# Turning B and C of eight pairs with crossbar DMAs on the sync queue instead of TensorE transposes

## The chip, the cores and the metric

The kernel runs on one core of one Trainium2 chip. The metric is the device time of one execution, in microseconds (us), as the median of several executions. With one core there is no second die to compare with, so an execution counts as "slow" when it is over 1.5% above the fastest of the same kernel. Comparisons use the others, the "fast" ones. Every ratio below is the mean time of one kernel's fast runs over the mean time of the other's fast runs of the same rounds, so it is not quite the ratio of the medians that stand beside it.

A profiled execution has a span a little shorter than the device time (125.4 us against 127.1). All times read from profiles count from the start of that span.

## The reference

A state-space layer (Mamba-2 style, in chunks) is followed by a gated feed-forward layer. Cut to what matters here:

```python
x: (4, 8, 768, 32)   a: (4, 8, 768)   B, C: (4, 8, 768, 16)    # batch, heads, tokens, ...
for each chunk of tokens:
    CB      = C @ B^T                      # per head, tokens x tokens
    y_intra = (CB * L) @ x                 # L: causal decays
    y_inter = (C @ state) * decay
    state   = decay_full * state + B^T @ (x * decay)
y -> 3072 tokens x 256
out = (relu(y @ w_gate) * (y @ w_val)) @ w_out     # 256 -> 1536 -> 256
```

`CB` sums over the 16 state columns, and a matmul sums over partitions. So B and C, loaded with tokens on the partitions, have to be turned until head and state lie on the partitions.

## The kernel before

The 3072 tokens are cut into 12 pairs of 128-token chunks and into 6 blocks of 512 tokens. Attention of pair P = 2b+2 and Q = 2b+3 is woven into the feed-forward matmuls of block b. Each engine works through its instructions in program order, and so does the sync queue (SP), which issues nearly all DMAs. The parts that matter:

```python
def load(p):                         # six DMAs on the sync queue for pair p >= 3
    q = nc.sync
    ...
    for i in range(2):               # two chunks
        for src, j in ((B, 0), (C, 1)):
            q.dma_start(out=bcr[:, i, j], in_=src[b, :, sl, :].rearrange("h s n -> s h n"))
        q.dma_start(out=xr[:, i], in_=x[b, :, sl, :].rearrange("h s d -> s h d"))

def scale_bc(p, eng):                # GpSimd: decay factors into B and C, cast to bf16
    bs = att.tile([128, 4, 128], BF16, tag="bs", name="bs")
    for t in range(2):
        eng.tensor_tensor(out=bs...[:, :, t], in0=src[:, :, t], in1=f..., op=ALU.mult)
    s["tin"] = [[bs[:, 2 * i + j] for i in range(2)] for j in range(2)]

def transp(p, k):                    # TensorE: two 128x128 transposes of B (k=0) or C (k=1)
    for i in range(2):
        nc.tensor.transpose(out=s["tp"][k][:, i], in_=s["tin"][k][i], identity=ident)

def tevac(p, beng, ceng):            # PSUM -> SBUF: BT, and CT twice (t=0,1), with half of
    (...copy)(BT, tp[0])             # the head slots zeroed by tmask
    ... out_[:, t] = tok * tmask[:, t]

def inter(p, i):                     # y_inter: the first TensorE user of CT in a block
    for t in range(2):
        nc.tensor.matmul(out=s["y"][:, t, i], lhsT=Sm[:, t], rhs=s["CT"][:, t, i], ...)

for b in range(1, NBLK):
    P, Q, W = 2 * b + 2, 2 * b + 3, 2 * b + 1
    for n in (P + 2, P + 3):         # loads of the pairs of the NEXT block
        if n < NPAIR:
            load(n)
    ...                              # gvh(): gate and val of half blocks
    for f in range(n, NF):
        gv(b, f)                     # gate and val matmuls, ScalarE relu, VectorE product
        if at("scale P"...): scale(P, nc.gpsimd, nc.gpsimd)       # b = 1 only
        if at("scale Q"...): scale(Q, nc.gpsimd, nc.gpsimd)
        if at("scale next P"...): scale(P + 2, nc.gpsimd, nc.gpsimd)
        if at("turn P"...): turn(P); tevac(P, nc.scalar, nc.vector)
        if at("turn Q"...): turn(Q); tevac(Q, nc.scalar, nc.scalar)
    inter(P, 0)
    fout(b, 0)                       # o matmuls
    G(P); sums(P); gevac(P); ...     # CB of pair P, and its causal masks
```

Of the kernel before, what the change touches and what calls it, by code (L numbers as in the profile page):

```python
# [9 lines left out]
BF16 = mybir.dt.bfloat16  # L10
AF = mybir.ActivationFunctionType
ALU = mybir.AluOpType
# [17 lines left out]
def kernel(  # L30
# [13 lines left out]
    nc = tc.nc  # L44

    NB, NH, S, D = x.shape
    N = B.shape[-1]
# [10 lines left out]
    glob = ctx.enter_context(tc.tile_pool(name="glob", bufs=1))  # L58
    raw = ctx.enter_context(tc.tile_pool(name="raw", bufs=4))
    att = ctx.enter_context(tc.tile_pool(name="att", bufs=3))  # L60
# [42 lines left out]
    def load(p):  # L103
        q = nc.sync
        if p < NWIDE:
            load_bc(p, 1, q)
            load_bc(p, 0, q)
            load_x(p, q)
            return
        b, c0 = p // PPB, 2 * (p % PPB)  # L110
        xr = raw.tile([128, 2, NH, D], FP32, tag="xr", name="xr")
        bcr = raw.tile([128, 2, 2, NH, N], FP32, tag="bcr", name="bcr")
        for i in range(2):
            sl = slice((c0 + i) * 128, (c0 + i + 1) * 128)
# [3 lines that stand above are left out]
        st[p] = {"xr": xr, "bcr": bcr}  # L118
# [27 lines left out]
    for rows, base in ((slice(0, 128), 128), (slice(0, 64), 0)):  # L146
        nc.gpsimd.affine_select(
            out=wmask[rows], in_=wmask[rows], pattern=[[-1, 2], [1, 128]],
# [6 lines left out]
    for k in range(4):  # L155
# [16 lines left out]
        out=cp0, data0=a0, data1=zero1[0:R].to_broadcast([R, 128]), initial=1.0,  # L172
# [32 lines left out]
    def factors():  # L205
        d = bank("fac", (128, 2, NH, PPB))
        for r in range(2):
            for i in range(2):
                nc.tensor.matmul(
                    out=d[64 * i:64 * i + 64, r].rearrange("p h k -> p (h k)"),  # L210
                    lhsT=cp0[:, r:128:2], rhs=idr[:, i:R:2], start=(r == 0), stop=True,
                    tile_position=(0, 64 * i), skip_group_check=True)
        return d
# [24 lines left out]
    scaleBC = glob.tile([128, NB, NC, 2, 8], FP32)  # L238
# [30 lines left out]
    def scale_wide(p, j, eng):  # L269
# [6 lines left out]
        for t in range(2):  # L276
# [4 lines left out]
                in1=f[:, :, 4 * t:4 * t + 4].to_broadcast([128, 2, 4, N]),  # L281
                op=ALU.mult)

    def scale_bc(p, eng):
        b, c0 = p // PPB, 2 * (p % PPB)
        s = st[p]
        bs = att.tile([128, 4, 128], BF16, tag="bs", name="bs")
        src = s["bcr"].rearrange("s i j (t q) n -> s (i j) t q n", t=2)
        f = scaleBC[:, b, c0:c0 + 2].rearrange("s c j h -> s (c j) h")
        for t in range(2):  # L290
            eng.tensor_tensor(  # L291
                out=bs.rearrange("s k (q t n) -> s k t q n", q=4, t=2)[:, :, t],
                in0=src[:, :, t],
                in1=f[:, :, 4 * t:4 * t + 4].to_broadcast([128, 4, 4, N]),
                op=ALU.mult)
        s["tin"] = [[bs[:, 2 * i + j] for i in range(2)] for j in range(2)]
        s["B"] = s["tin"][0]
# [12 lines left out]
    def transp(p, k, apart=False):  # L310

        s = st[p]
        if "tp" not in s:
            s["tp"] = {}
        if apart and k == 0:
            s["tp"][k] = bank("tpb", (128, 2, 128), BF16)
        elif not s["tp"]:
            tp = mm.tile([128, 2, 2, 128], BF16, tag="tp", name="tp")
            s["tp"] = {0: tp[:, 0], 1: tp[:, 1]}
        for i in range(2):  # L320
            nc.tensor.transpose(out=s["tp"][k][:, i], in_=s["tin"][k][i], identity=ident)  # L321

    def tevac(p, beng, ceng):

        s = st[p]
        tp = s.pop("tp")
        s["BT"] = BT = att.tile([128, 2, 128], BF16, tag="BT", name="BT")
        s["CT"] = CT = att.tile([128, 2, 2, 128], BF16, tag="CT", name="CT")
        wide = p < NWIDE

        tok, out_ = tp[1], CT
        if wide:
            tok = tok.rearrange("s r m -> s m r")
            out_ = out_.rearrange("s t i m -> s t (i m)").rearrange("s t (m r) -> s t m r", r=2)
        if p > 1:
            (beng.copy if beng is nc.scalar else beng.tensor_copy)(BT, tp[0])
        if ceng is nc.scalar:
            for t in range(2):
                nc.scalar.mul(out_[:, t], tok, tmask[:, t:t + 1])
        else:  # L340
            shape = [128, 2] + list(tok.shape[1:])
            nc.vector.tensor_tensor(
                out=out_, in0=tok.unsqueeze(1).to_broadcast(shape),
                in1=tmask.unsqueeze(2).unsqueeze(3).to_broadcast(shape), op=ALU.mult)
        if p < 2:
            (beng.copy if beng is nc.scalar else beng.tensor_copy)(BT, tp[0])
# [230 lines left out]
    def yevac(p, eng):  # L577
        s = st.pop(p)
        dst = yT[:, :, p * 256:(p + 1) * 256]
        src = s["y"].rearrange("r t i m -> r t (i m)")  # L580
        if eng is nc.scalar:
            eng.copy(out=dst, in_=src)  # L582
        else:
            eng.tensor_copy(dst, src)
# [18 lines left out]
    def gvh(b, f, u, later=False):  # L603

        if f == 0 and u == 0:
            fst[b] = ffn.tile([128, NF, 512], BF16, tag="h", name="h")
        tk = slice(b * 512 + u * 256, b * 512 + (u + 1) * 256)
        fs = slice(f * 128, (f + 1) * 128)
        gv_ = bank("gv", (128, 2, 256))
        for j, w in ((0, wg), (1, wv)):  # L610
            for k in range(2):
                nc.tensor.matmul(out=gv_[:, j], lhsT=w[:, k, fs], rhs=yT[:, k, tk],  # L612
                                 start=(k == 0), stop=(k == 1), skip_group_check=True)
        r = ffn.tile([128, 512], BF16, tag="r", name="r", bufs=5)[:, 0:256]
        nc.scalar.activation(r, gv_[:, 0], AF.Relu)  # L615

        def finish():
            nc.vector.tensor_tensor(out=fst[b][:, f, u * 256:(u + 1) * 256], in0=r,  # L618
                                    in1=gv_[:, 1], op=ALU.mult)

        if later:
            return finish
        finish()
# [59 lines left out]
    def turn(p, apart=False):  # L683
        transp(p, 1, apart)
        transp(p, 0, apart)
# [4 lines left out]
    d = factors()  # L690
# [47 lines left out]
    def halves(b, u, *fs):  # L738
        for f in fs:
            gvh(b, f, u)  # L740
# [84 lines left out]
    yevac(3, A_)  # L825
    halves(1, 0, 4, 5)

    for b in range(1, NBLK):
        P, Q, W = 2 * b + 2, 2 * b + 3, 2 * b + 1
        more = P < NPAIR  # L830
        for n in (P + 2, P + 3):
            if n < NPAIR:
                load(n)

        def at(name, *fs):

            return more and f == fs[min(b, len(fs) - 1)]

        n = 6 if b == 1 else 4
        if b > 1:  # L840
            for f in range(n):
                gvh(b, f, 0)
                if f == 1:
                    inter(W, 0)
                    inter(W, 1)
                    Dm(W)
                    if more:
                        sums(P)
                    yevac(W, nc.scalar)
                    if more:  # L850
                        states(P)
        for f in range(n):
            gvh(b, f, 1)
        for f in range(n, NF):
            gv(b, f)
            if b == 1 and at("scale P", 99, 6):
                scale(P, nc.gpsimd, nc.gpsimd)
            if at("scale Q", 9, 6, 4):
                scale(Q, nc.gpsimd, nc.gpsimd)
            if at("scale next P", 11, 11, 9) and P + 2 < NPAIR:  # L860
                scale(P + 2, nc.gpsimd, nc.gpsimd)
            if at("turn P", 9, 6, 5):
                turn(P)
                tevac(P, nc.scalar, nc.vector)
            if at("turn Q", 99, 8, 8):
                turn(Q)
                tevac(Q, nc.scalar, nc.scalar)
        if more:
            inter(P, 0)
            if b > 1:  # L870
                inter(P, 1)
        fout(b, 0)
        foevac(b, 0)
        if more:
            G(P)
            if b == 1:
                sums(P)
            gevac(P)
            if b == 1:
                states(P)  # L880
        fout(b, 1)
        foevac(b, 1)
        fout(b, 2)
        foevac(b, 2)
        if more:
            if b == 1:
                inter(P, 1)
            Dm(P)
            sums(Q)
            yevac(P, nc.scalar)  # L890
            G(Q)
            gevac(Q)
            states(Q)
        fout(b, 3)
        foevac(b, 3)
# [32 lines left out]
```

## Time and profile before

The median is 127.81 us (127.36 to 128.01, four runs).

| engine | busy, of a span of 125.4 us |
|---|---|
| TensorE (PE) | 119.2 us, 95% |
| VectorE (DVE) | 88.3 us, 70% |
| ScalarE (ACT) | 82.0 us, 65% |
| GpSimd (POOL) | 42.3 us, 34% |

A busy share alone doesn't say what bounds a kernel. The chain of work that ended last does: it starts from the last instruction and goes back, at each step, to what released it. Here is a piece of it, from the kernel before (columns: start in us, length in us, engine, tile and line, number of instructions):

```profile
39.17 0.43 PE val L597 x2
39.60 0.22 PE tp L321 x4
39.83 0.43 PE gate L594 x2
...
43.94 0.43 PE val L597 x2
44.37 0.11 PE y L558 x2
44.48 1.31 PE o L639 x12
45.79 0.33 PE g L481 x8
...
46.35 2.73 PE o L639 x24
...
49.91 1.42 PE o L639 x12
51.33 0.77 PE gv L612 x7
```

Each piece begins where the one before it ends. That holds from 24.97 us to 122.6 us, so in that stretch a microsecond counts only if TensorE spends it. The four transposes of a pair (`tp`) take 0.22 us of the chain, and `y L558` at 44.37 us is the first matmul of block 1 that needs pair 4's CT.

The groups of the same kernel that turn B and C (line, engine, operation, shapes, count, then busy time and mean ns of one, then idle time before them):

```profile
L321 PE MATMUL tp<-ident,bs 128*128 128x128 bf16 x44 | 4.4, 220 | 0.2 <-DVE bs L277 0.2
L339 ACT ACTIVATE CT<-tp,tmask 128x256 bf16<-128x256 bf16 x10 | 4.2, 479 | 0.0
L342 DVE TENSOR_TENSOR CT<-tp,tmask 128x512 bf16<-128x512 bf16 x6 | 4.1, 685 | 0.2 <-ACT BT L336 0.2
L336 ACT COPY BT<-tp 128x256 bf16<-128x256 bf16 x9 | 3.4, 372 | 0.5
```

A mean of 220 ns for a transpose isn't its price on TensorE: matmuls overlap, and the chain gives 0.22 us for four.

What the sync queue does around block 1, in order of time (start, length of the issue, instruction; the loads from 38.85 us on are those of pairs 6 and 7):

```profile
35.82 1.80 SPq L117 DMA_DIRECT2D xr<-in_x_dram  x1
37.72 1.04 SPq L679 DMA_DIRECT2D out_dram<-ob  x2
38.85 0.44 SPq L116 DMA_DIRECT2D bcr<-in_B_dram  x1
...
46.87 0.85 SPq L117 DMA_DIRECT2D xr<-in_x_dram  x1
51.98 0.38 SPq L657 DMA_DIRECT2D out_dram<-ob  x1
```

The queue is busy issuing without a break until 47.72 us, and no engine is shown waiting for one of these loads: they are for the next block. It then idles until the store of block 1.

### The profile page before, as it was taken

How to read it: one execution, taken by the hardware profiler on the slowest of the kernel's cores; microseconds unless marked ns; L12 is line 12 of the kernel's file. 1: busy time of each engine (PE TensorE's matmuls, PEld its weight loads, DVE VectorE, ACT ScalarE, POOL GpSimd, SP SyncE). 2: the span in 40 equal slices, each digit the busy share in tenths (PEclk: the TensorE clock that was granted, in tenths of full speed). 3: DMA queues.
4: the chain of work that ended last, by engine and by line, in shares of the span. 5: the costliest groups of instructions: out<-in, count | busy, mean ns of one | idle time of the engine just before them, and what ended most of it. 6: DMA issues, size and time to landing. Idle time of an engine off the chain costs nothing.

```text
span 125.4 us, 3648 instructions
## 1 busy us (share of the span) xinstructions
PE 119.2 (95%) x1400; PEld 83.2 (66%) x1400; DVE 88.3 (70%) x196; ACT 82.0 (65%) x185; POOL 42.3 (34%) x86
## 2 busy tenths in 40 slices
PE   6879799899999999999999999999999999999990
PEld 6656585378686578874477865577864577854790
DVE  4795888754799675998673899664989655687510
ACT  0568588835788843787945787935887745876410
POOL 6599863127445016800511801421700033000000
PEclk9999999999999999999999999999999999999999
DMA  3999999987898999196950399920400002200022
GB/s 66 215 172 204 172 216 197 144 106 90 95 105 222 113 116 98 44 200 75 120 70 0 104 167 112 98 40 0 156 16 0 0 0 89 84 0 0 0 89 84
DMA packets 72305, 12.15 MB, mean 97 GB/s; under 512 B 65904, under 2 KB 72288, under 8 KB 72288
## 3 DMA queue, kind: packets, MB, share of 16 engines
q1 hardware_dynamic: 66048, 8.84, 47.9%
q0 software_dynamic: 3184, 2.36, 12.6%
q10 hardware_dynamic: 3056, 0.72, 2.7%
q8 instruction: 11, 0.18, 0.6%
q14 instruction: 6, 0.05, 0.1%
HBM read 11.13 MB, written 3.15 MB: 114 GB/s over the span
## 4 chain that ended last, share of the span: by engine, by line
PE 83%; DMA 9%; ACT 2%; DVE 1%; issue 1%; POOL 1%; DVEq 0%; POOLq 0%
PE o L639 25%; PE gv L612 16%; PE val L597 13%; PE gate L594 13%; DMA wo<-in_moe_w_out_dram 9%; PE w L180 2%; PE y L569 2%; PE g L481 2%; PE tp L321 2%; PE y L558 1%; ACT gs L389 1%; PE o L633 1%; PE g L372 1%; POOL gs L385 1%; PE A_ps L528 1%
## 5 line engine op out<-in xcount | busy, mean ns | idle before, releaser
L601 DVE TENSOR_TENSOR h<-r,val 128x512 bf16<-128x512 bf16 x44 | 29.5, 686 | 8.8 <-ACT r L600 7.2
L639 PE MATMUL o<-wo,h 128*128 128x256 bf16 x276 | 32.8, 273 | 0.5 <-DMA wo<-in_moe_w_out_dram 0.5
L600 ACT ACTIVATE r<-gate 128x512 bf16<-128x512 f32 x44 | 25.9, 600 | 6.0 <-PE gate L594 4.0
L639 PEld LDWEIGHTS <-h 128*128 128x128 bf16 x276 | 25.9, 98 | 5.6 <-issue 1.5
L597 PE MATMUL val<-yT,wv 128*128 128x512 bf16 x88 | 26.2, 379 | 0.0
L594 PE MATMUL gate<-yT,wg 128*128 128x512 bf16 x88 | 26.2, 379 | 0.0
L618 DVE TENSOR_TENSOR h<-r,gv 128x256 bf16<-128x256 bf16 x56 | 22.5, 418 | 2.7 <-ACT r L615 1.8
L615 ACT ACTIVATE r<-gv 128x256 bf16<-128x256 f32 x56 | 21.4, 385 | 2.5 <-PE gv L612 0.4
L612 PE MATMUL gv<-yT,wv 128*128 128x256 bf16 x112 | 21.4, 273 | 0.7 <-DMA wv<-in_moe_w_val_dram 0.7
L612 PE MATMUL gv<-yT,wg 128*128 128x256 bf16 x112 | 21.4, 273 | 0.1
L506 DVE TENSOR_TENSOR gs<-g,maskUT 128x512 bf16<-128x512 f32 x18 | 11.6, 686 | 11.7 <-issue 9.6
L489 POOL TENSOR_SCALAR_AFFINE_SELECT gs<-gs 128x512 bf16<-128x512 bf16 (+1 forms) x18 | 9.0, 523 | 31.3 <-ACT gs L500 31.3
L291 POOL TENSOR_TENSOR bs<-bcr,scaleBC 128x256 bf16<-128x256 f32 x18 | 11.0, 633 | 21.3 <-PE gate L594 6.3
L597 PEld LDWEIGHTS <-wv 128*128 128x128 bf16 x88 | 8.6, 98 | 10.4
L594 PEld LDWEIGHTS <-wg 128*128 128x128 bf16 x88 | 8.2, 98 | 7.0
L612 PEld LDWEIGHTS <-wv 128*128 128x128 bf16 x112 | 10.9, 98 | 2.2 <-DMA wv<-in_moe_w_val_dram 0.9
L612 PEld LDWEIGHTS <-wg 128*128 128x128 bf16 x112 | 10.2, 98 | 2.0 <-issue 0.2
L500 ACT CAST gs<-g 128x512 bf16<-128x512 f32 x9 | 5.3, 589 | 6.7 <-PE g L481 6.7
L582 ACT CAST yT<-y 128x512 bf16<-128x512 f32 x9 | 5.3, 586 | 5.3 <-PE y L569 2.7
L180 PE MATMUL w<-warm 128*128 128x128 bf16 x49 | 5.0, 265 | 1.1 <-DVE tmask L154 1.1
L540 DVE TENSOR_TENSOR Sm<-A_ps,smask 128x256 bf16<-128x256 f32 x15 | 5.7, 415 | 0.0
L180 PEld LDWEIGHTS <-warm 128*128 128x128 bf16 x58 | 4.6, 118 | 1.7 <-DVE tmask L154 1.0
(108 smaller groups left out, 120.6 us busy)
## 6 DMA issues: line engine op xcount, KB each, us to landing
xr<-in_x_dram SPq DMA_DIRECT2D x19, 128.0 KB, 3.8
out_dram<-ob SPq DMA_DIRECT2D x3, 512.0 KB, 3.1
bcr<-in_C_dram SPq DMA_DIRECT2D x19, 64.0 KB, 3.5
bcr<-in_B_dram SPq DMA_DIRECT2D x19, 64.0 KB, 3.7
out_dram<-ob SPq DMA_DIRECT2D x4, 256.0 KB, 2.4
wo<-in_moe_w_out_dram POOLq DMA_DIRECT2D x1, 768.0 KB, 11.0
xr<-in_x_dram SPq DMA_DIRECT2D x2, 256.0 KB, 8.1
wg<-in_moe_w_gate_dram POOLq DMA_DIRECT2D x1, 384.0 KB, 6.2
```

The lines of the kernel that those rows point to most:

```text
L180: nc.tensor.matmul(out=w, lhsT=warm, rhs=rhs, start=True, stop=True)
L291: eng.tensor_tensor(out=bs.rearrange("s k (q t n) -> s k t q n", q=4, t=2)[:, :, t], in0=src[:, :, t], in1=f[:, :, 4 * t:4 * t + 4].to_bro ...
L489: nc.gpsimd.affine_select(out=dst, in_=dst, pattern=[[0, n], [1, 128]], compare_op=ALU.is_ge, fill=0.0, base=0, channel_multiplier=-1)
L506: nc.vector.tensor_tensor(out=d[:, q], in0=g[q], in1=m, op=ALU.mult)
L594: nc.tensor.matmul(out=g, lhsT=wg[:, k, fs], rhs=yT[:, k, tk], start=(k == 0), stop=(k == 1))
L597: nc.tensor.matmul(out=v, lhsT=wv[:, k, fs], rhs=yT[:, k, tk], start=(k == 0), stop=(k == 1))
L600: nc.scalar.activation(r, g, AF.Relu)
L601: nc.vector.tensor_tensor(out=fst[b][:, f], in0=r, in1=v, op=ALU.mult)
L612: nc.tensor.matmul(out=gv_[:, j], lhsT=w[:, k, fs], rhs=yT[:, k, tk], start=(k == 0), stop=(k == 1), skip_group_check=True)
L615: nc.scalar.activation(r, gv_[:, 0], AF.Relu)
L618: nc.vector.tensor_tensor(out=fst[b][:, f, u * 256:(u + 1) * 256], in0=r, in1=gv_[:, 1], op=ALU.mult)
L639: nc.tensor.matmul(out=o[:, ts % 2], lhsT=fst[b][:, f, ts * 128:(ts + 1) * 128], rhs=wo[:, f], start=(f == 0), stop=(f == NF - 1), skip_gr ...
```

## The change

The intent is to take the turning of pairs 4 to 11 off TensorE. GpSimd writes scaled B and C into one of four tiles of 128 tokens by six slots. Two slots are B; the other four are C twice, each time with half of its head slots never written, so they keep the zeros of one early memset. One crossbar DMA per pair (a DMA that transposes blocks of 128x128 while it copies) then turns all six slots, which yields BT and the masked CT at once. The diff, cut at one spot:

```diff
+    FIRST = 4
+    NTOK = 4
+    tok = [glob.tile([128, 6, 128], BF16, name="tok%d" % i) for i in range(NTOK)]
     def scale_bc(p, eng):
         b, c0 = p // PPB, 2 * (p % PPB)
         s = st[p]
+        if p >= FIRST:
+            bs = tok[p % NTOK]
+            ... (views of source, factors, destination)
+            for t in range(2):
+                for j in range(2):
+                    eng.tensor_tensor(
+                        out=dst[:, t, j * (1 + t)], in0=src[:, j, :, t],
+                        in1=f[:, j, :, 4 * t:4 * t + 4].to_broadcast([128, 2, 4, N]),
+                        op=ALU.mult)
+            turned = att.tile([128, 6, 128], BF16, tag="turned", name="turned", bufs=4)
+            nc.sync.dma_start_transpose(out=turned, in_=bs.rearrange("s k c -> s (k c)"))
+            s["B"] = [bs[:, i] for i in range(2)]
+            s["BT"] = turned[:, 0:2]
+            s["CT"] = turned[:, 2:6].rearrange("s (t i) m -> s t i m", t=2)
+            return
@@ before the loop over blocks
+    for t in tok:
+        nc.gpsimd.memset(t, 0.0)
@@ in the loop over blocks
-            if at("turn P", 9, 6, 5):
-                turn(P)
-                tevac(P, nc.scalar, nc.vector)
-            if at("turn Q", 99, 8, 8):
-                turn(Q)
-                tevac(Q, nc.scalar, nc.scalar)
```

More of the change, by code (lines that the diff above doesn't have):

```diff
@@ L286, in scale_bc @@
         s = st[p]
+        if p >= FIRST:
+            bs = tok[p % NTOK]
+            src = s["bcr"].rearrange("s i j (t q) n -> s j i t q n", t=2)
+            f = scaleBC[:, b, c0:c0 + 2].rearrange("s c j h -> s j c h")
+            dst = bs.rearrange("s (j i) (q t n) -> s t j i q n", i=2, q=4, t=2)
+            for t in range(2):
[10 more added lines that the diff above has]
+            return
         bs = att.tile([128, 4, 128], BF16, tag="bs", name="bs")
```

## The prediction

> **What bounds the kernel now.** TensorE: busy 119.2 of 125.4 us (the page's busy table). In the chain of work that ended last its pieces follow one another without a gap from 24.97 to 122.6 us, so there only TensorE time counts. VectorE (88.3), ScalarE (82.0) and GpSimd (42.3) have room.
>
> **Removed.** Four TensorE transposes of each of pairs 4 to 11. Four cost 0.22 us in the chain: 8 x 0.22 = 1.76 us, all on the critical path, and the whole possible gain (1.4%). Also the evictions: a BT copy (372 ns) per pair, and a CT product on VectorE (685 ns) or two on ScalarE (479 ns each). They are off the chain and worth nothing.
>
> **Added.** On GpSimd four memsets of 128x768 after pair 3's causal masks (about 0.75 us each, an estimate from 128x128 at 0.20 us and 128x256 at 0.31), and four 128x128 scalings (0.41 us) instead of two of 128x256 (0.62), 0.4 us more per pair; it has that idle time. And eight crossbar transposes of 192 KB on the sync queue. The trace has none to read. The Trainium skill ("VectorE: DVE Perf Modes", The three transpose paths) gives 1309 ns for one 128x128 through the crossbar; six blocks are between that and 7.9 us. I take 4.5 us to land on a free ring (estimate).
>
> **What decides: order on the sync queue.** In block 1 the loads of pairs 6 and 7 come first, then the transposes of pairs 4, 5, 6. In the sync queue's timeline those loads are issued without a break up to 47.7 us. But TensorE wants pair 4's CT at 44.20 us (the first y<-CT,Sm matmul of that block; 43.8 with eight transposes gone), and GpSimd will have scaled pair 4 by about 39 us: the transpose is ready 9 us before it is issued. Then it stands behind loads in flight (DMA busy until about 50 us). I expect it to land at about 53 us: TensorE, in order, stands still for about 9.5 us, and nothing gives that back.
>
> Such a gap probably cools the clock. The skill ("TensorE: Matmul & The Clock Gate", Part 1) says that an idle window of about 3.4 us halves the clock until about 3.4 us of work have passed. The trace agrees at the start: 22 warm-up matmuls of 128 columns took 2.51 us, 114 ns each, against 55 later. Estimate: +1.7 us.
>
> Pair 7's transpose stands behind the loads of pairs 8 and 9: issued about 11 us after block 1's output store, landing at +16.5, wanted by G(7) at +15.4: 1.1 us more. Pair 9 is about even (+15.6 against +15.5). The others have slack.
>
> **Sum.** -1.8 + 9.5 + 1.7 + 1.1 = +10.5 us: 138.5 us, range 133 to 150. Faster by over 2%: 1%; within 2%: 6%; slower: 93%.
>
> **What would show it.** Right: one long wait of TensorE for the DMA of the turned tile near 44 us, ending at 51 to 55; the first transpose issued right after pair 7's last load, near 47.7; matmuls after the gap at double time; waits of 0 to 2 us at G(7), G(9); VectorE down by 2.7 and ScalarE by 6.8 us, without effect. Wrong: no such wait, or equal waits in each block.
>
> **What would make it wrong.** Transposes far slower than 4.5 us, or serialised against the loads: then pairs 5, 7 and 9 stall too, to 150 us and more. Loads issued earlier than before, or a transpose landing in 2 us: 133 to 135.

## More of the kernel before

The start of the kernel varies from execution to execution: TensorE's turn of pair 3, which no experiment edits, came between 30.11 and 31.25 us in the kept traces. So where two traces are compared to a tenth, they are compared from one point, TensorE's turn of pair 3 near 30 us, to the end.

## The result, and the profile after

The changed kernel takes 135.53 us in the median (134.37 to 135.74, four runs), against 127.81 us. The ratio is 1.059, with a 95% interval of 1.052 to 1.066. It is slower, and correct.

The groups that waited longest, as far as TensorE and its weight loads are concerned, in the changed kernel (who waited for whom: total us, times, longest):

```profile
PEld L582 <- DMA turned<-tok: 8.4, 1, 8.4
PE y L582 <- DMA turned<-tok: 7.9, 1, 7.9
```

It is one wait, once. The chain of the changed kernel, from just ahead of it to the first matmuls of the next block (to be laid beside the piece of before; the `o` matmuls are now line 663):

```profile
43.95 0.59 SPq L116
...
47.05 0.67 SPq L116
...
47.77 1.10 SPq L117
...
48.96 3.12 DMA turned<-tok
...
52.13 0.39 PE y L582 x2
52.53 2.56 PE o L663 x12
55.09 0.55 PE g L505 x7
...
55.97 3.06 PE o L663 x24
...
59.86 1.42 PE o L663 x12
61.28 0.87 PE gv L636 x8
```

Ahead of the wait the chain no longer runs through TensorE. It runs through the sync queue, which is busy issuing loads (lines 116 and 117), and then through the transpose that had to stand behind them. And after the wait the same matmuls take longer: 12 `o` matmuls 2.56 us instead of 1.31, the next 24 3.06 instead of 2.73.

The sync queue and GpSimd of the changed kernel at the same time:

```profile
39.31 0.46 SPq L116 DMA_DIRECT2D bcr<-in_B_dram  x1
...
47.77 1.10 SPq L117 DMA_DIRECT2D xr<-in_x_dram  x1
48.96 3.98 SPq L306 DMA_TRANSPOSE turned<-tok  x3
61.92 0.39 SPq L681 DMA_DIRECT2D out_dram<-ob  x1
```

```profile
34.35 2.77 POOL L853 MEMSET tok<- 128x768 bf16 x4
37.09 1.49 POOL L301 TENSOR_TENSOR tok<-bcr,scaleBC 128x128 bf16<-128x128 f32 x4
38.52 0.62 POOL L331 CAST xb<-xr 128x512 bf16<-128x512 f32 x1
39.09 1.49 POOL L301 TENSOR_TENSOR tok<-bcr,scaleBC 128x128 bf16<-128x128 f32 x4
```

GpSimd has pair 4 ready at 38.58 us. Its transpose is issued at 48.96 us, 10.4 us later and 0.09 us after the last load of pair 7.

The granted clock, which is the share of its full clock that TensorE was given, in steps of about 1 us (columns: stretch, its length, then busy time of PE, PEld, DVE, ACT and POOL with counts, then granted TensorE clock, DMA share, GB/s):

```profile
45.00:46.00 1.00, 0.00 (x0) 0.00 (x0) 0.17 (x1) 0.00 (x0) 0.73 (x2) 1.00 0.91 119
46.00:47.00 1.00, 0.00 (x0) 0.00 (x0) 0.00 (x0) 0.00 (x0) 0.79 (x3) 0.69 1.03 96
...
53.00:54.00 1.00, 1.00 (x6) 0.72 (x5) 0.00 (x0) 0.00 (x0) 0.00 (x0) 0.50 1.00 192
...
55.50:56.00 0.50, 0.50 (x21) 0.35 (x18) 0.21 (x1) 0.28 (x1) 0.11 (x1) 0.50 0.00 0
56.00:57.00 1.00, 1.00 (x7) 0.77 (x7) 1.00 (x3) 0.57 (x2) 1.00 (x2) 0.69 0.00 0
```

Stretches wholly ahead of the fall and wholly behind it show 1.00 and 0.50. A clock that averages 0.69 over a microsecond was at 0.5 for 0.62 of it. So it fell at about 46.4 us (46 + 0.38), 2.1 us after TensorE had stopped at 44.24, and rose at about 56.6 us (56 + 0.62), 4.5 us after TensorE had started again. With finer steps the two points are 46.38 and 56.62, which makes 10.24 us at half clock.

The account, from the turn of pair 3 to the end: 95.02 us before (125.4 - 30.38), 103.30 us after (134.0 - 30.70), so +8.28 us. The wait is 7.88 us. The slow clock is 2.19 us: from the first `y` matmul of block 1 to the first `gv` of the next takes 9.15 us (52.13 to 61.28) instead of 6.96 (44.37 to 51.33). The removed transposes are -1.76 us. The sum is +8.31. The 2.19 us are those of the profiled execution, whose mean clock (0.962) is the lowest of the four. The other three had 0.974, which answers to about 7.0 us at half clock instead of 10.24 (an estimate: 0.026 x 133.8 / 0.5). How much of that fell on work isn't on record.

The other transposes cost nothing here: TensorE waits for none of them. In the changed kernel the eight take 1.25 us of the sync queue each and land 2.8 to 4.4 us after issue, 3.0 in the median.

### The profile page after: what moved, and what is told of

Same layout as the page of the kernel before. It is cut to its first block, busy times and chain, and to the rows that moved or that the text cites. A ratio compares the mean times of both kernels' runs of the same rounds, so it can differ in the third digit from the quotient of the medians.

```text
span 134.0 us, 3583 instructions
## 1 busy us (share of the span) xinstructions
PE 119.7 (89%) x1362; PEld 82.6 (62%) x1368; DVE 86.8 (65%) x192; ACT 77.0 (57%) x169; POOL 47.3 (35%) x106
## 4 chain that ended last, share of the span: by engine, by line
PE 71%; DMA 11%; SPq 5%; POOL 5%; issue 3%; ACT 2%; DVE 0%; DVEq 0%; POOLq 0%
PE o L663 25%; PE gv L636 11%; PE val L621 11%; PE gate L618 10%; DMA wo<-in_moe_w_out_dram 8%; PE w L180 3%; SPq L116 3%; PE g L505 2%; DMA turned<-tok 2%; SPq L117 2%; PE y L593 2%; POOL tok L301 2%; POOL tok L853 2%; PE y L582 1%; ACT gs L413 1%
## 5 line engine op out<-in xcount | busy, mean ns | idle before, releaser
L625 DVE TENSOR_TENSOR h<-r,val 128x512 bf16<-128x512 bf16 x44 | 30.3, 688 | 8.6 <-ACT r L624 7.9
L663 PE MATMUL o<-wo,h 128*128 128x256 bf16 x276 | 34.5, 281 | 0.3 <-DMA wo<-in_moe_w_out_dram 0.3
L663 PEld LDWEIGHTS <-h 128*128 128x128 bf16 x276 | 26.7, 101 | 6.2 <-issue 1.5
L618 PE MATMUL gate<-yT,wg 128*128 128x512 bf16 x82 | 24.9, 379 | 0.0
L513 POOL TENSOR_SCALAR_AFFINE_SELECT gs<-gs 128x512 bf16<-128x512 bf16 (+1 forms) x18 | 8.9, 521 | 30.9 <-ACT gs L524 30.9
L301 POOL TENSOR_TENSOR tok<-bcr,scaleBC 128x128 bf16<-128x128 f32 x32 | 12.0, 404 | 16.2 <-DMA bcr<-in_B_dram 5.1
L582 PE MATMUL y<-turned,Sm 128*128 128x128 bf16 x28 | 3.2, 225 | 7.9 <-DMA turned<-tok 7.9
L331 POOL CAST xb<-xr 128x512 bf16<-128x512 f32 x9 | 5.5, 611 | 9.3 <-PE A_ps L552 9.1
L582 PEld LDWEIGHTS <-Sm 128*128 128x128 bf16 x30 | 2.3, 99 | 9.6 <-DMA turned<-tok 8.4
```

Of the source, the lines that this page charges most:

```text
L301: eng.tensor_tensor(out=dst[:, t, j * (1 + t)], in0=src[:, j, :, t], in1=f[:, j, :, 4 * t:4 * t + 4].to_broadcast([128, 2, 4, N]), op=ALU. ...
L513: nc.gpsimd.affine_select(out=dst, in_=dst, pattern=[[0, n], [1, 128]], compare_op=ALU.is_ge, fill=0.0, base=0, channel_multiplier=-1)
L618: nc.tensor.matmul(out=g, lhsT=wg[:, k, fs], rhs=yT[:, k, tk], start=(k == 0), stop=(k == 1))
L625: nc.vector.tensor_tensor(out=fst[b][:, f], in0=r, in1=v, op=ALU.mult)
L663: nc.tensor.matmul(out=o[:, ts % 2], lhsT=fst[b][:, f, ts * 128:(ts + 1) * 128], rhs=wo[:, f], start=(f == 0), stop=(f == NF - 1), skip_gr ...
```

## The experiments

**The theory.** The added work is cheap, but it is placed where the sync queue can't get to it: pair 4's transpose is written behind twelve loads. The rest is the clock. **Rivals:** GpSimd delivers the data late (memsets, four smaller scalings); the crossbar transposes are slow, or slow beside loads; or the added work itself loads the memories.

### Nothing turned: what the removal alone is worth

The kernel before, with a wrong result: constant tiles in place of the turned ones.

```diff
             if at("turn P", 9, 6, 5):
-                turn(P)
-                tevac(P, nc.scalar, nc.vector)
+                st[P]["BT"], st[P]["CT"] = BTc, CTc
             (the same for Q)
```

> Wrong result on purpose: the kernel before with the 32 TensorE transposes of pairs 4 to 11 and their evictions taken out and constant tiles read in their place. It measures what the removal is worth where nothing replaces it. By the chain of before, 8 x 0.22 = 1.76 us: 126.05 us, ratio 0.986. If the evictions on ScalarE and VectorE were worth something too, it is faster than 125.5.

Measured: 125.75 us against 127.23 of before on the same chip, ratio 0.987 (0.982 to 0.992). From the turn of pair 3 to the end it is 93.22 us, 1.80 less than before. So the removal is worth what the chain said, 1.76 us, and the evictions, though VectorE and ScalarE are busy for 1.3 and 5.2 us less, are worth nothing.

### Everything added, nobody waits for it

The kernel before, still turning on TensorE, with the memsets, the scalings into the six-slot tiles and the eight DMA transposes as work that nobody reads.

```diff
     def scale_bc(p, eng):
+        if p >= FIRST:
+            (scale into tok[p % NTOK], start the DMA transpose, as in the change, without return)
         bs = att.tile([128, 4, 128], BF16, tag="bs", name="bs")
```

> The kernel before, with everything that the change adds (memsets, the four-piece scalings, the eight crossbar transposes at the same place of the sync queue) as extra work that nobody reads; TensorE still turns B and C. GpSimd does both scalings, so it has more work than in the changed kernel. Order theory: additions cost nothing unless TensorE waits for them: 127.8 us, within 0.7. Rival (the added work itself slows the kernel, on GpSimd, in the DMA engines or in the memories): several us slower, 131 or more.

Measured: 129.15 us against 127.23, ratio 1.013 (1.008 to 1.018). That missed the expectation of "within 0.7", though it is far from the 7.7 us of the change. From the turn of pair 3 to the end it is 96.25 us, 1.23 more than before, and one wait of TensorE explains 1.03 of it:

```profile
43.49 0.40 PE L338 MATMUL tp<-ident,bs 128*128 128x128 bf16 x4 [1.03 <-POOL bs L308]
```

GpSimd scales twice in this kernel, so TensorE waited for its scaled pair 5. That is a fault of the experiment, since the changed kernel scales once. It leaves some 0.2 us for everything else that was added. The timed runs differ by a little more, 1.7 us between the means of the fast ones. In the profiled run TensorE's turn of pair 3 was 0.87 us late as well, because the load of `w_out` landed later; that is ahead of all that was added, and the other runs have no trace.

### Block 1's loads behind the transposes of pairs 4 and 5

The changed kernel; only the order of twelve loads and two transposes on the sync queue is altered. GpSimd's work and the size of the transposes stay.

```diff
         for n in (P + 2, P + 3):
-            if n < NPAIR:
+            if n < NPAIR and b > 1:
                 load(n)
...
                 scale(Q, nc.gpsimd, nc.gpsimd)
+                if b == 1:
+                    load(P + 2)
+                    load(P + 3)
```

> Block 1's twelve loads (pairs 6 and 7) are issued after the transposes of pairs 4 and 5 instead of before them; nothing else differs from the changed kernel. Order theory: the first transpose is issued as soon as GpSimd has scaled pair 4, near 38.7 us, and lands near 41.8, before TensorE wants it at 43.8; the 7.9 us wait and the halved clock both go, and 126.3 us remain (126.0 to 127.2, ratio 0.985 to 0.995); pair 7's transpose may cost a few tenths. Rivals (GpSimd's memsets and smaller scalings make the data late; or crossbar transposes are slow beside loads): the wait stays and the time is above 133 us.

Measured: 127.25 us against 127.23, ratio 0.999 (0.995 to 1.003). The long wait and the half clock are gone (mean granted clock 1.0 in the profile), which no rival allowed for. But the time is a microsecond above the 126.3 expected. Pair 4's transpose is issued at 38.75 us, and TensorE has a new wait:

```profile
50.11 0.65 PE L593 MATMUL y<-gs,xb 128*32 128x128 bf16 x16 [1.36 <-POOL gs L513]
```

`gs L513` are the causal masks of pair 4. GpSimd, in order, has the scaling of pair 6 ahead of them, and that scaling stood 6.5 us waiting for pair 6's load, which now comes later. So most of the gain of 1.76 us was spent on a new wait of 1.4 us: moving the loads back made the next thing late that depends on them.

### Only pair 7's loads behind: a half dose

```diff
-            if n < NPAIR:
+            if n < NPAIR and (b > 1 or n == P + 2):
                 load(n)
...
                 scale(Q, nc.gpsimd, nc.gpsimd)
+                if b == 1:
+                    load(P + 3)
```

> Only pair 7's six loads go behind the transposes of pairs 4 and 5; pair 6's six stay ahead. Order theory, dose: pair 6's loads are issued until about 43.9 us, the first transpose then lands about 3.1 us later, near 47.0; TensorE waits about 3.1 us instead of 7.9[...], so 126.05 + 3.1 = 129.2 us (128.5 to 130.5). A rival that is not about the loads ahead expects no change from 135.5.

Measured: 128.93 us against 127.43, ratio 1.008 (1.002 to 1.013). The transpose is issued at 43.26 us, right behind pair 6's last load, and TensorE waits 2.25 us (3.1 were expected):

```profile
46.72 0.29 PE L582 MATMUL y<-turned,Sm 128*128 128x128 bf16 x2 [2.25 <-DMA turned<-tok]
```

Twelve loads ahead give a wait of 7.9 us, six give 2.25, none gives none: the wait follows the loads. The clock stays at 1.0 in the profiled run. Of the six timed runs three had a mean clock of 1.0 (127.7 to 128.7 us) and three 0.987 (129.1 to 130.9 us). A clock of 0.987 answers to about 3.3 us at half speed (an estimate: 0.013 x 128.3 / 0.5), a third of the 10.24 us above. So the slow clock may come or not with a wait of this size. That isn't shown: there are no traces of these three, two of them count as slow, and the kernel with block 1's loads behind, which doesn't have this wait in its trace, also has a slow run at 0.987.

### Filling the wait with warm-up matmuls

To separate the clock from the wait, 125 matmuls of 128 columns were put where TensorE waits.

```diff
+        if b == 1:
+            keep_warm(125)
         if more:
             inter(P, 0)
```

> The changed kernel with 125 warm-up matmuls of 128 columns (about 6.95 us at 55.6 ns) put ahead of the matmul that waits, so that TensorE works through most of the 7.9 us. Clock theory: the granted clock stays 1.0, the twelve o matmuls after the wait take 1.31 us again instead of 2.56, and the time falls by about 1.9 us to 133.6. Rival (they were slow for another reason, such as the DMA traffic of the transposes): no change, 135.5.

Measured: 135.29 us against 127.43, ratio 1.051 (1.046 to 1.057), but three of the six runs counted as slow and the times ran from 133.4 to 137.2, so it was run again, beside the changed kernel on one chip.

> The changed kernel, unaltered, on the same chip as the run with the filled wait, to measure the clock's share. 135.5 us, ratio to before about 1.06, granted clock 0.96 to 0.975.

> The kernel with the wait filled by 125 warm-up matmuls, again, beside the changed kernel on one chip. In the first run's trace the twelve o matmuls after the wait took 1.47 us instead of 2.77 and the stretch from the first y<-turned,Sm to the next block's gv took 6.97 us instead of 9.15, but the executions were spread over 133.4 to 137.2 us. Clock theory: fast runs 1 to 2.2 us below the changed kernel on this chip, granted clock 1.0 against 0.97. Rival: no difference.

Measured: the changed kernel 134.81 us, ratio to before 1.057 (1.053 to 1.061), clock 0.962 to 0.975; with the filled wait 134.62 us, ratio 1.056 (1.052 to 1.060), clock 1.0 in every run. In total no difference. In the trace the clock's share is plain: the chain of the kernel with the filled wait has the matmuls at their old length again.

```profile
48.39 4.09 DMA turned<-tok
52.53 0.29 PE y L582 x2
52.82 1.31 PE o L663 x12
...
59.67 0.87 PE gv L636 x8
```

From the first `y` to the next `gv` it takes 7.14 us here and 9.58 us in the changed kernel of the same rounds, 2.44 us less. The profile also shows where that went. Pair 4's transpose took 4.1 us to land instead of 3.4, and the wait ended 0.7 us later, counted from the turn of pair 3. In block 3 a wait of 0.87 us appears for pair 9's transpose: it was issued 11.7 us after the store of block 2 instead of 10.4, and took 4.6 us to land instead of 3.2. From the turn of pair 3 to the end that leaves 102.28 us against 103.12. So 2.2 to 2.4 us of slow clock are shown in the traces as the length of the same matmuls at half and at full clock; that removing it makes the kernel as much faster is not shown. One part of the reason may be that both traces of the changed kernel are of executions at 0.962, while all its other runs had 0.974 or 0.975, and so less of the slow clock to remove. Why those transposes landed later in the kernel with warm-up matmuls stays open.

### The transposes on ScalarE's queue

```diff
-            nc.sync.dma_start_transpose(...)
+            nc.scalar.dma_start_transpose(...)
```

> The changed kernel with the eight transposes issued from ScalarE's queue, which has no loads; the loads stay where they are on the sync queue. Order theory: the transpose of pair 4 starts near 38.6 us and lands near 42; the long wait and the slow clock go. The price is 1.25 us of ScalarE for each issue and ScalarE's wait for GpSimd's scaling, so some short waits: 126 to 129 us. Rival (a crossbar transpose is held up by the loads in the DMA engines, not by the queue): a wait of several us stays and it is above 132.

Measured: 139.14 us against 127.43, ratio 1.087 (1.083 to 1.092): slower still, a miss. ScalarE's queue in that run:

```profile
39.14 0.60 ACT L624 ACTIVATE r<-gate 128x512 bf16<-128x512 f32 x1
45.08 2.63 ACTq L306 DMA_TRANSPOSE turned<-tok  x2
47.81 1.57 ACT L624 ACTIVATE r<-gate 128x512 bf16<-128x512 f32 x3 [8.07 <-issue]
```

The transpose was not issued near 38.6 us but at 45.08, and until then ScalarE did nothing. TensorE soon stood still for 6.8 us, waiting, in its `val` matmuls, for ScalarE's relu, which frees the PSUM bank that they write. The instruction listing of the built program shows what held the transpose. A DMA here has one of eight semaphores in turn, and waits for the last user of its own. For pair 4's transpose that is the second C load of pair 6. That load was issued at 41.44 us and took 3.6 us to land: 45.04 us. The Trainium skill ("DMA: Bandwidth & Descriptors", Anatomy of one DMA) says, in its account of GpSimd's DMAs, that DMA engines don't wait on semaphores and that any such wait happens on the issuing sequencer. This run agrees: ScalarE, behind its sequencer, idled for 8.07 us, of which 5.3 were the wait (39.74 to 45.08 us) and the rest the issue of two transposes. So another queue didn't free the transpose from the loads, and it made ScalarE wait with it.

To test the semaphore, the loads of pairs 6 and 7 were written after the transposes in the program, with the transposes still on ScalarE's queue (the edits of the two runs together):

> The transposes on ScalarE's queue as in the earlier run, but in the program the loads of pairs 6 and 7 are written after the transposes of pairs 4 and 5. The sync queue still issues those loads at the same time as before, since it holds nothing else between. Theory of the shared semaphores: in the earlier run the transpose of pair 4 was held until 45.1 us because each DMA waits for the landing of the eighth DMA written before it, there a load of pair 6; now that is an old one, so it starts near 39 us (when GpSimd has scaled pair 4), and the 6.8 us wait of TensorE for ScalarE shrinks to 0 to 2 us: 127 to 130 us. Rival (the transposes on this queue are slow or late because the loads fill the DMA engines): it still starts near 45 us, or lands as late, and the time stays at 137 to 140.

Measured: 139.45 us against 127.54, ratio 1.092 (1.087 to 1.096). It is no test. The built program has the same instructions in the same order, with the same waits, on every engine as the run before, so it repeats that run, and the transpose still waits for the same load (issued at 41.38 us, landed 3.8 us later at 45.18; the transpose was issued at 45.22). Twice the landing and the issue agree to 0.04 us, but no run took the semaphore away, so that part is argued and not shown. What these two runs exclude is only that a second queue by itself is the cure.

### The transposes ahead of loads in every block, memsets early

```diff
-        for n in (P + 2, P + 3):
-            if n < NPAIR:
-                load(n)
...
                 scale(Q, nc.gpsimd, nc.gpsimd)
+                for n in (P + 2, P + 3):
+                    if n < NPAIR:
+                        load(n)
(and the four memsets moved into GpSimd's idle time near 20 us)
```

> Candidate: in every block the loads are issued after the transposes of pair Q (so also those of pair 7 and 9 go ahead of loads), and the four memsets stand earlier, in GpSimd's wait for a load near 20 us. Order theory: no wait of TensorE for a transpose anywhere, 126.0 us (125.7 to 126.6), equal to the run with nothing turned within 0.5 us. If loads delayed by 2 to 3 us make another pair late, a new wait of GpSimd and then of TensorE shows and it is slower than 127.

Measured: 127.23 us (125.99 to 127.84 in fast runs) against 127.23, ratio 0.9975 (0.992 to 1.003), a miss of the 126.0 expected. No transpose is waited for. What is left is the wait of the block 1 run, shorter (0.61 us), for the masks of pair 4.

### And pair 6 scaled after the masks of pair 4

```diff
-            if at("scale next P", 11, 11, 9) and P + 2 < NPAIR:
+            if b > 1 and at("scale next P", 11, 11, 9) and P + 2 < NPAIR:
                 scale(P + 2, nc.gpsimd, nc.gpsimd)
...
             gevac(P)
             if b == 1:
+                scale(P + 2, nc.gpsimd, nc.gpsimd)
                 states(P)
```

> The candidate with one more move: in block 1 GpSimd scales pair 6 after the causal masks of pair 4 instead of before them. The candidate's trace showed one new wait: TensorE's y<-gs,xb of pair 4 waited 0.61 us for those masks, because GpSimd stood for the load of pair 6 that now comes later. If that was all that ate the gain, the wait goes and the whole 1.76 us of the removed transposes is left: from pair 3's turn to the end 93.3 us (before 95.0, candidate 94.2), ratio to before 0.986. If not, another wait appears and it stays at the candidate's 0.9975.

Measured: 125.75 us (125.40 to 126.05) against 127.54, ratio 0.987 (0.984 to 0.989). From the turn of pair 3 to the end it is 93.27 us (123.7 - 30.43). That is the 93.22 us of the kernel in which nothing was turned at all: the whole of the removed transposes, and all that could be had. Its sync queue, to be laid beside the two above:

```profile
37.95 1.04 SPq L703 DMA_DIRECT2D out_dram<-ob  x2
39.08 2.70 SPq L306 DMA_TRANSPOSE turned<-tok  x2
41.83 0.58 SPq L116 DMA_DIRECT2D bcr<-in_B_dram  x1
```

Same work as in the changed kernel, in another order on two in-order queues: 9 us less. This version is correct. It beats the changed kernel by far, and the kernel before by 1.3%, clear of the noise.

## Why the prediction was right

- **What bounds it, and what removal is worth: right.** TensorE's chain has no gap from 25 us on. The predicted 1.76 us is confirmed by the kernel with nothing turned (1.80) and by the reordered one (1.75). That the evictions are worth nothing held too. Their effect on busy time was put too high, 2.7 us on VectorE and 6.8 on ScalarE against 1.5 and 5.0: the groups that were removed did shrink nearly as forecast (CT on VectorE from 4.1 to 1.4 us; BT and CT on ScalarE from 7.6 to 1.2), but busy times of groups overlap, so the engines' busy time shrank by less: VectorE's `h` products, still 44 of them, went from 29.5 to 30.3 us.
- **The added GpSimd work: right.** A memset took 742 ns (estimated 0.75 us), and the data of pair 4 was ready at 38.58 us ("by about 39").
- **The step that decided, order on the sync queue: right, and shown by experiment.** The transpose was issued 0.09 us after pair 7's last load (48.96 us; 47.7 was read from a trace whose loads ended 1.2 us earlier). Taking loads from ahead of it changes the wait from 7.9 to 2.25 to none, with all the added work in place.
- **The size of the wait: 9.5 us predicted, 7.9 measured.** The term that was off is the landing. It was put at about 5.3 us after the issue, with 4.5 us on a free ring and loads in flight ahead; it was 3.1 us. The later issue (1.3 us) hid a part of this error, and TensorE came 0.4 us later than forecast. The figure came from the Trainium skill's 1309 ns for one 128x128 block ("VectorE: DVE Perf Modes", The three transpose paths), stretched toward six blocks; six blocks in one DMA land in 3.0 us in the median, less than the 4.5 of the estimate. How the time grows with the number of blocks isn't shown, since no run turned another number.
- **The clock: 1.7 us predicted, 2.2 measured.** The mechanism holds as the skill tells it ("TensorE: Matmul & The Clock Gate", Part 1), but for the time of the fall (see the last section): the record shows 0.5, and twelve `o` matmuls took 2.56 us instead of 1.31. It lasted 4.5 us of work rather than 3.4. In the executions at 0.974 the slow stretch was shorter; what it cost them isn't shown.
- **Pair 7: 1.1 us predicted, none measured; pair 9 "about even": nearly.** Pair 7's transpose was issued 11.2 us after the store, as predicted, but landed at +14.4 instead of +16.5, ahead of G(7) at +15.4. The same landing term was too large. The margin is a microsecond, and in both profiles with the filled wait pair 9's transpose did come late (0.87 us, and 1.43 in a slow run).
- **The sum** of +10.5 us was +7.7 us in the medians, inside the range of 133 to 150 us, but near its lower end: the wait and pair 7 were both put too high, by the same landing term, and the clock too low.

## What to carry to other kernels

When work moves from an engine to a DMA, first ask what stands ahead of it on the queue that issues it, and when: a queue that nobody waits for may be full of loads for later, and the first thing with a deadline put behind them inherits all their issue time. Put the urgent DMA ahead of the loads, then look for what the delayed loads feed in order (here GpSimd's scaling, ahead of masks that TensorE wanted): moves of order alone (the loads, the memsets, one scaling) turned +6% into -1.3%. A gap on TensorE can also cost more than its length: after the 7.9 us gap the clock stood at half for 4.5 us of work, while the profiled run with a gap of 2.25 us kept 1.0. The Trainium skill's advice to issue a DMA early and wait on it late ("DMA: Bandwidth & Descriptors", Rules for kernel authors) is only as good as the place in the queue: here the wait was late, and the issue was too.

## What the Trainium skill lacked or had wrong

- "VectorE: DVE Perf Modes" gives a time for one 128x128 block through the crossbar; no page that we found gives one for several blocks in one DMA on this chip (only bandwidths). Measured: a transpose of 128x768 bf16 takes 1.25 us of the issuing queue and lands 3.0 us after issue in the median (2.8 to 4.4 in the changed kernel; on ScalarE's queue 4.7, with 2.8 to 6.7).
- "TensorE: Matmul & The Clock Gate" puts the fall of the clock after at least one idle window of about 3.4 us, a window that runs freely. In the changed kernel it fell about 2.1 us after TensorE stopped and came back 4.5 us after it started again. The free-running window agrees with the traces: between two changes of the clock the changed kernel's record has 40.96, 10.24 and 78.51 us, which are 12, 3 and 23 times 3.413. But if a window ends where the clock changes, the one that ended with the fall (42.97 to 46.38 us) still held 1.27 us of work, so it was not idle throughout; how much work it may hold isn't shown. With a wait of 2.25 us the profiled run kept 1.0, while three of six timed runs had 0.987.
- "DMA: Bandwidth & Descriptors" tells where a DMA's semaphore wait happens, but not what such a wait does on a compute engine's queue: with the transposes on ScalarE's queue, ScalarE idled 8.07 us (5.3 of them the wait) and the kernel was 9% slower than before.
